# Attention products in plain float32 on halves and strips of the array, two heads at once

## The chip, the cores and the metric

The kernel runs on one core of one Trainium2 chip. The metric is the device time of one execution in microseconds (us). TensorE (PE in the profile) multiplies matrices, VectorE (DVE), ScalarE (ACT) and GpSimd (POOL) work on elements, SyncE (SP) issues the transfers between device memory and the on-chip buffers. PSUM is the on-chip memory that TensorE's products land in; it has eight banks of 512 float32 values on each of 128 partitions.

## The reference

The first stage is a linear attention with a feature map, for 8 batches of 8 heads with 576 tokens, a head width of 64 and 128 features. Its result is reshaped to 4608 tokens of 512 values, and a gated layer with 1536 inner columns follows.

```python
def phi(x):
    proj = np.einsum('bhsd,df->bhsf', x, w_phi)
    proj = proj - np.max(np.abs(proj), axis=-1, keepdims=True)
    return np.concatenate([np.exp(proj), np.exp(-proj)], axis=-1)
q_p, k_p = phi(q), phi(k)
kv = np.einsum('bhsf,bhsd->bhfd', k_p, v)
z = np.sum(k_p, axis=2)
num = np.einsum('bhsf,bhfd->bhsd', q_p, kv)
den = np.einsum('bhsf,bhf->bhs', q_p, z)[..., None] + 1e-06
x = (num / den).transpose(0, 2, 1, 3).reshape(B * S, H * D)
a = x @ w_a
b = x @ w_b
out = a * b @ w_out
```

## The kernel before, in words

The work has two phases. In the first, the attention of 32 pairs of heads (8 batches, 4 pairs each) is interleaved with the first pass of the gated layer, which takes 6 of its 12 slices of inner columns over 12 blocks of 384 tokens (`moe_block`, products at L609 and L632). The second pass (`second_pass`, L722 and L833) takes the other 6 slices in blocks of 768 tokens with a scheme that trades products for sums; it begins when the first pass is done, and the change doesn't touch it. A block of the first pass needs the normalised attention of the tokens in it, from all heads of a batch.

A product can be made in two ways. In plain float32 each product appears in the trace as two records of TensorE, each with a weight load of its own. In the split way an operand is cut into a rounded part and the rest (`split`, `stack`, type float32r), the product is the sum of three products of such parts (`products`), and each has one record. The gated layer is split everywhere. The attention is plain for the first pairs (`PLAIN_K, PLAIN_Q, PLAIN_KV, PLAIN_NUM = 9, 6, 11, 9` at L45: keys up to pair 9, queries up to 6, and so on) and split for the rest. ScalarE and VectorE make the parts (L153, L160, L165).

For a pair of heads the steps are these. `features` projects the keys: 4 chunks of 128 tokens, and a fifth of 64 tokens that two pairs share (`rest_chunk`). In the plain way one product per chunk makes both heads, with a weight matrix that holds w_phi twice and zeros elsewhere, 256 columns (L234); in the split way there are two products per chunk, where the low part lies in the other half of the rows (L243). VectorE takes the largest absolute value and subtracts it (L248, L249), ScalarE makes two exponentials (L257, L258). `kv_add` (L300) multiplies the values by these features and adds over the chunks in one PSUM bank; a column of ones beside the 64 value columns makes z in the same product, so that the stationary operand is 65 columns wide, and 64 in the product of the values' low part. `k_finish` copies the sums out and transposes them by four products (L322). `q_side` does the queries head by head: two products of 288 tokens each (L358), the largest absolute value over the partitions on POOL (L362), exponentials (L366, L367), and products with the transposed sums, numerator and denominator in one, again 65 columns wide (L382). Numerators go to device memory (`xun`), denominators too (`den`). `reciprocals` loads the denominators, inverts them, stores them, loads them again spread over the partitions (`rb`), loads the numerators (`x32` from `xun`), multiplies (L410), and stores `xnorm`, from which the blocks load.

The order of the source is set by turns. `attention_steps` gives each step of a pair a turn (5 turns from pair to pair for the first 7 pairs, 4 after that), sorts the steps by turn, and between turns `run` issues steps of the gated layer and of the weight decoding at 0.65 or 0.75 steps per turn. The instructions of each engine are then put in order by a scheduler with a model of times (`schedule_with_timeline_sim=True`), so TensorE's order isn't that of the source. The four attention buffers in PSUM (tag `att`) are one bank each, three banks belong to the gated layer (tag `moe`), and one to the sums.

## Time and profile before

| what | value |
|---|---|
| median of 3 runs | 1219.85 us |
| lowest and highest run | 1218.25 and 1220.84 us |
| span of the profiled execution | 1218.5 us |
| PE busy | 1182.0 us, 97% |
| DVE busy | 972.3 us, 80% |
| ACT busy | 779.0 us, 64% |
| DMA busy share, from 100 to 694 us | 0.50 |

The span runs from the first instruction to the last of one execution; what the profiled execution took as a whole isn't listed beside it, and the median of the runs is 1.35 us above the span. Attention products run from 4 us to 694 us, products of the first pass from 65 us to 803 us, those of the second pass from 806 us on. TensorE's records are pipelined: the next one starts before the one before it ends, so what a product costs in a row of products is the distance between starts, not the duration of a record.

### The profile page before, as it was taken

Reading aid. Unit: us, or ns where it says so; the run is one execution under the profiler, and the core shown is the slowest. Engines: PE = TensorE matmul, PEld = TensorE weight load, DVE = VectorE, ACT = ScalarE, POOL = GpSimd, SP = SyncE. Lnnn points to the kernel's source line nnn. Section 1 sums busy time; section 2 is a strip of 40 time slices with the busy share of each in tenths; the row PEclk is TensorE's granted clock in tenths of the full one; section 3 lists DMA queues with packets and bytes.
Section 4 is the critical chain, followed back from the end, with each engine's and each line's share of the span. In section 5 each row is a group of like instructions: output and inputs, shape, how many; then the busy total and the mean of one; then the engine's idle time right before and its main releaser. Section 6 shows DMA issues by size and latency. Waiting matters only on the chain.

```text
span 1218.5 us, 20169 instructions
## 1 busy us (share of the span) xinstructions
PE 1182.0 (97%) x7086; PEld 1125.7 (92%) x7086; DVE 972.3 (80%) x1716; ACT 779.0 (64%) x1656; POOL 152.5 (13%) x69
## 2 busy tenths in 40 slices
PE   8889999999999999999999999999999999999998
PEld 5557888999999999999999999999999999998997
DVE  7966988898898889898888479978768595867665
ACT  6767778888888888888788445644345353535332
POOL 2222222121221221131122000000000000000000
PEclk9999999999999999999999999999999999999999
DMA  8665664454455454545341578759586767768572
GB/s 254 206 208 179 181 189 130 133 167 119 140 154 159 116 166 114 161 131 170 108 132 55 168 251 298 236 169 309 174 271 204 232 240 219 257 205 285 169 247 87
DMA packets 120949, 225.21 MB, mean 185 GB/s; under 512 B 21456, under 2 KB 58064, under 8 KB 120848
## 3 DMA queue, kind: packets, MB, share of 16 engines
q1 hardware_dynamic: 120400, 223.66, 59.2%
q8 instruction: 56, 0.92, 0.3%
q14 instruction: 45, 0.37, 0.1%
q10 hardware_dynamic: 448, 0.26, 0.1%
HBM read 174.81 MB, written 49.05 MB: 184 GB/s over the span
## 4 chain that ended last, share of the span: by engine, by line
PE 70%; DMA 13%; DVE 9%; ACT 5%; issue 2%; SPq 0%; DVEq 0%; ACTq 0%
PE po L833 9%; PE pa L722 9%; PE pa L609 9%; PE pb L722 9%; PE pb L609 8%; PE po L632 8%; PE kvps L300 7%; PE pn L382 6%; DMA x<-xnorm 3%; PE pq L358 2%; DMA back_w<-kept_w 2%; DMA xnorm<-x 1%; PE pk L243 1%; DMA rb<-rec 1%; DMA rec<-r 1%
## 5 line engine op out<-in xcount | busy, mean ns | idle before, releaser
L362 POOL PARTITION_ALL_REDUCE mb<-p x64 | 152.2, 2378 | 524.8 <-ACT p L359 412.0
L609 PE MATMUL pa<-xh,w_a 128*128 128x384 f32 x576 | 165.7, 341 | 5.7 <-ACT xh L153 4.1
L609 PE MATMUL pb<-xh,w_b 128*128 128x384 f32 x576 | 161.6, 338 | 0.0
L632 PE MATMUL po<-hh,w_o 128*128 128x384 f32 x576 | 153.1, 337 | 2.0 <-ACT o L644 2.0
L609 PEld LDWEIGHTS pa<-xh,w_a 128*128 128x128 f32 x576 | 105.6, 189 | 8.1 <-ACT xh L153 5.0
L632 PEld LDWEIGHTS po<-hh,w_o 128*128 128x128 f32 x576 | 104.1, 188 | 2.9 <-ACT o L644 2.6
L609 PEld LDWEIGHTS pb<-xh,w_b 128*128 128x128 f32 x576 | 105.0, 188 | 0.3
L609 PE MATMUL pa<-xl,w_a 128*128 128x384 f32 x288 | 98.1, 341 | 0.0
L609 PE MATMUL pb<-xl,w_b 128*128 128x384 f32 x288 | 97.1, 337 | 0.0
L632 PE MATMUL po<-hl,w_o 128*128 128x384 f32 x288 | 96.8, 338 | 0.3 <-DVE hl L160 0.3
L160 DVE TENSOR_TENSOR qel<-qe,qeh 128x1152 fp32r<-128x1152 f32 x46 | 62.9, 1366 | 28.1 <-ACT qeh L153 25.8
L833 PE MATMUL po<-hh_s,own_o 128*128 128x384 f32 x288 | 80.2, 335 | 0.6 <-DVE o L815 0.3
L165 DVE TENSOR_TENSOR qs<-q,qs 64x576 fp32r<-64x576 f32 x52 | 63.1, 1214 | 16.4 <-ACT qs L153 15.2
L383 ACT COPY xn<-pn 65x288 f32<-65x288 f32 x128 | 48.9, 395 | 23.1 <-PE pn L382 17.2
L833 PE MATMUL po<-hh_w,own_o 128*128 128x384 f32 x216 | 59.1, 334 | 0.0
L632 PEld LDWEIGHTS po<-hl,w_o 128*128 128x128 f32 x288 | 54.1, 188 | 0.8 <-DVE hl L160 0.7
L366 ACT ACTIVATE qe<-p 128x576 f32<-128x576 f32 x64 | 44.6, 696 | 15.9 <-DVE qel L160 12.2
L609 PEld LDWEIGHTS pa<-xl,w_a 128*128 128x128 f32 x288 | 54.2, 188 | 0.3
L609 PEld LDWEIGHTS pb<-xl,w_b 128*128 128x128 f32 x288 | 54.2, 188 | 0.3
L153 ACT CAST qeh<-qe 128x1152 fp32r<-128x1152 f32 x46 | 53.5, 1162 | 1.4 <-PE pn L382 1.3
L833 PEld LDWEIGHTS po<-hh_s,own_o 128*128 128x128 f32 x288 | 52.6, 188 | 1.5 <-DVE o L815 0.6
L257 ACT ACTIVATE ke<-kd 128x512 f32<-128x512 f32 x64 | 40.9, 640 | 20.1 <-DVE kd L249 19.4
(299 smaller groups left out, 3422.1 us busy)
## 6 DMA issues: line engine op xcount, KB each, us to landing
back_s<-kept_s SPq DMA_DIRECT2D x71, 512.0 KB
back_w<-kept_w SPq DMA_DIRECT2D x52, 512.0 KB
q<-in_qD SPq DMA_DIRECT2D x52, 288.0 KB
k<-in_km SPq DMA_DIRECT2D x55, 256.0 KB
xun<-xn SPq DMA_DIRECT2D x64, 144.0 KB
x<-xun SPq DMA_DIRECT2D x32, 288.0 KB
rb<-rec SPq DMA_DIRECT2D x32, 288.0 KB
xnorm<-x SPq DMA_DIRECT2D x32, 288.0 KB
```

What stands on the lines that cost most here:

```text
L153: eng.copy(dst, src)
L160: eng_lo.tensor_tensor(lo, src, hi, op=ALU.subtract)
L165: eng_lo.tensor_tensor(hi_lo[D:], src[D:], hi_lo[D:], op=ALU.subtract)
L300: nc.tensor.matmul(st["kv_ps", b, pr][:width, j], v_[:, j, :width], e_[:, j], start=(left == NFULL and j == 0 and n_ == 0), stop=(left == ...
L362: nc.gpsimd.partition_all_reduce(mb, p32, P, bass_isa.ReduceOp.absmax)
L366: nc.scalar.activation(e[:, 0], p32, AF.Exp)
L382: nc.tensor.matmul(pn[: D + 1, :HALF], kv_[:, 2 * j + s, :], e_[:, s, tok], **at)
L383: nc.scalar.copy(xn[: D + 1, tok], pn[: D + 1, :HALF])
L609: nc.tensor.matmul(acc, w[:, cc * P : (cc + 1) * P], x, start=(k == 0), stop=(k == 3 * NCC - 1))
L632: nc.tensor.matmul(accs[cc], w[:, cc * P : (cc + 1) * P], h, **at)
L722: in_turn(lambda: nc.tensor.matmul(acc[to][i], w_, x_, skip_group_check=True, **at), u.startswith("1_0"))
L833: in_turn(lambda: nc.tensor.matmul(acc[m, to], w_, h_, skip_group_check=True, **f), False)
```

## The change

All attention products become plain float32, for all pairs. They are laid on parts of the array. The projections of queries and keys have 64 contracted rows per head, so the two heads of a pair stand on the two halves of the rows (`heads[j]`) and write two PSUM banks. The sums over keys and values and the numerators have 64 output columns per head, so the two heads stand on the two halves of the columns. The column of ones goes: z is made by products with a stationary operand of 32 columns of ones, on four strips of 32 columns for two heads and two signs of the exponent (`strips`), from the features of all chunks for the first 8 pairs, and from their sum, which VectorE makes first (`summed`), for the other 24. Denominators are products of their own, on four strips for two heads and two halves of the tokens (`den_products`). The transposes become three of 128 x 128.

Each step is one function, issued in one turn: `load` at turn -5, `project` at 0, `summed` at 2, `kv_products` and `z_products` at 4, `turn` at 5, `num_products` and `den_products` at 8, with 4 turns between pairs. Steps of the same turn are sorted by kind, so in one turn come `project` of a pair, `kv_products` of the pair before, `num_products` of the one before that, then `z_products` and `den_products`. All products of attention and of the first pass go through `pe`, which ties each to the one before it, so that TensorE runs them in the order of the source. PSUM has two attention buffers of two banks instead of four of one; the sums and their transposes share one bank, and the three banks of the gated layer stay. The numerators of a pair are copied to `x32` on chip and stay there until they are multiplied; `xun` goes. The splits of keys, queries, values and features go, and so do the loads of the doubled queries (`qD`) and of the values with a column of ones. The rows of x come in the order of the heads, and the host lays the weights out to fit.

The core of the diff:

```diff
-TURNS0, TURNS, PAIRS0 = 5, 4, 7
...
+TURNS = 4
+LOAD_TURN, QK_TURN, SUM_TURN, KV_TURN, TURN_TURN, NUM_TURN = -5, 0, 2, 4, 5, 8
+SUM_FROM = 8
...
-PACE0, PACE, PACE0_UNTIL = 0.65, 0.75, 30
+PACE0, PACE, PACE0_UNTIL = 0.65, 0.75, 24
...
-PLAIN_K, PLAIN_Q, PLAIN_KV, PLAIN_NUM = 9, 6, 11, 9
...
-        ps = c.enter_context(tc.tile_pool(name="ps_att", bufs=4, space=PSUM))
+        ps = c.enter_context(tc.tile_pool(name="ps_att", bufs=2, space=PSUM))
...
+    ordered = [None]
+    def pe(issue):
+        ins = issue()
+        if ordered[0] is not None:
+            tc.add_manual_dep(
+                ins.ins,
+                ordered[0].ins.name,
+                mybir.DependencyInfo(mybir.DependencyClass.NoSync, mybir.DependencyReason.DATA),
+                reason="order of products",
+            )
+        ordered[0] = ins
+        return ins
+    def mm(out, w, x, start=True, stop=True):
+        return pe(lambda: nc.tensor.matmul(out, w, x, start=start, stop=stop, skip_group_check=True))
...
+        ones = a1.tile([P, 3, D // 2], F32, name="ones")
+        nc.vector.memset(ones, 1.0)
+        nc.vector.memset(ones[D:, 1], 0.0)
+        nc.vector.memset(ones[:D, 2], 0.0)
...
+    heads = [slice(j * D, (j + 1) * D) for j in range(2)]
+    strips = [slice(i * P // 4, (i + 1) * P // 4) for i in range(4)]
+    times = [slice(t * HALF, (t + 1) * HALF) for t in range(2)]
+    def load(b, pr, a1, a2, ps, consts, st):
         u = f"{b}_{pr}"
+        k32 = a2.tile([P, NFULL * P], F32, tag="k32", name=f"k32_{u}")
+        loads.append(nc.sync.dma_start(k32, km[b, pr]))
+        q32 = a2.tile([P, S], F32, tag="q32", name=f"q32_{u}")
+        loads.append(nc.sync.dma_start(q32, qP[b, pr]))
+        if pr % 2 == 0:
+            g = pr // 2
+            rk = a2.tile([P, P], F32, tag="rk", name=f"rk_{u}")
+            loads.append(nc.sync.dma_start(rk, kr[b, g]))
+            rv = a2.tile([P, 2, 2, D], F32, tag="rv", name=f"rv_{u}")
+            loads.append(nc.sync.dma_start(rv, vr[b, g]))
+            st["rk", b, g], st["rv", b, g] = rk, rv
+        v32 = a2.tile([P, NFULL, 2, D], F32, tag="v32", name=f"v32_{u}")
+        loads.append(nc.sync.dma_start(v32, vm[b, pr]))
+        st["k", b, pr], st["q", b, pr], st["v", b, pr] = k32, q32, v32
+    def features(u, y, n, a1, a2):
+        p = y if n == NFULL else y[:, :, :F]
+        p = p.rearrange("p j (c f) -> p j c f", f=F)
+        tag, bufs = ("d", 2) if n == NFULL else ("dr", 1)
+        d = a1.tile([P, 2, n, F], F32, tag=tag, bufs=bufs, name=f"d_{u}")
+        m = a2.tile([P, 2, n], F32, tag=f"m{n}", name=f"m_{u}")
+        nc.vector.tensor_reduce(out=m, in_=p, op=ALU.max, axis=AX.X, apply_absolute_value=True)
+        nc.vector.tensor_tensor(d, p, m.unsqueeze(3).broadcast_to([P, 2, n, F]), op=ALU.subtract)
+        e = a1.tile([P, 2, n, 2, F], F32, tag=f"e{n}", bufs=1 if n == NFULL else 2, name=f"e_{u}")
+        nc.scalar.activation(e[:, :, :, 0], d, AF.Exp)
+        nc.scalar.activation(e[:, :, :, 1], d, AF.Exp, scale=-1.0)
+        return e
+    def project(b, pr, a1, a2, ps, consts, st):
+        w2 = consts[0]
+        u = f"{b}_{pr}"
+        k32, q32 = st["k", b, pr], st["q", b, pr]
+        p32 = a2.tile([P, 2, S], F32, tag="p32", name=f"p32_{u}")
+        def q_half(t):
+            x = ps.tile([P, 2, 512], F32, tag="att", name=f"pq_{u}_{t}")
+            for j in range(2):
+                mm(x[:, j, :HALF], w2[heads[j]], q32[heads[j], times[t]])
+            return x
+        x = q_half(0)
+        nc.scalar.copy(p32[:, :, times[0]], x[:, :, :HALF])
+        y = ps.tile([P, 2, 512], F32, tag="att", name=f"pk_{u}")
+        for c in range(NFULL):
+            for j in range(2):
+                mm(y[:, j, c * P : (c + 1) * P], k32[heads[j], c * P : (c + 1) * P], w2[heads[j]])
+        x = q_half(1)
+        if pr % 2 == 0:
+            for j in range(2):
+                mm(x[:, j, HALF : HALF + F], st["rk", b, pr // 2][heads[j]], w2[heads[j]])
+        nc.scalar.copy(p32[:, :, times[1]], x[:, :, :HALF])
+        st["e", b, pr] = features(u, y, NFULL, a1, a2)
+        if pr % 2 == 0:
+            st["er", b, pr // 2] = features(f"r_{u}", x[:, :, HALF:], 1, a1, a2)
+        eq = a1.tile([P, 2, 2, S], F32, tag="eq", bufs=2, name=f"eq_{u}")
+        for j in range(2):
+            mb = a2.tile([P, S], F32, tag="mb", name=f"mb_{u}_{j}")
+            nc.gpsimd.partition_all_reduce(mb, p32[:, j], P, bass_isa.ReduceOp.absmax)
+            marks.append(nc.vector.tensor_tensor(p32[:, j], p32[:, j], mb, op=ALU.subtract))
+        nc.scalar.activation(eq[:, :, 0], p32, AF.Exp)
+        nc.scalar.activation(eq[:, :, 1], p32, AF.Exp, scale=-1.0)
+        st["eq", b, pr] = eq
+    def summed(b, pr, a1, a2, ps, consts, st):
+        if b * NPAIR + pr < SUM_FROM:
+            return
+        u = f"{b}_{pr}"
+        e, er = st["e", b, pr], st["er", b, pr // 2]
+        two = a1.tile([P, 2, 2, 2 * F], F32, tag="raw", bufs=2, name=f"two_{u}")
+        ev = e.rearrange("p j c s f -> p j c (s f)")
+        nc.vector.tensor_tensor(two, ev[:, :, 0:2], ev[:, :, 2:4], op=ALU.add)
+        z = st["z", b, pr] = a2.tile([P, 2, 2 * F], F32, tag="z", name=f"z_{u}")
+        nc.vector.tensor_tensor(z, two[:, :, 0], two[:, :, 1], op=ALU.add)
+        rows = heads[pr % 2]
+        rv = er.rearrange("p j c s f -> p j (c s f)")
+        nc.vector.tensor_tensor(z[rows], z[rows], rv[rows], op=ALU.add)
+    def kv_products(b, pr, a1, a2, ps, consts, st):
+        e, er = st["e", b, pr], st["er", b, pr // 2]
+        v32, rv = st["v", b, pr], st["rv", b, pr // 2]
+        kv = st["kv", b, pr] = ps.tile([P, 3, P], F32, tag="kv", bufs=1, name=f"kv_{b}_{pr}")
+        kvs = kv.rearrange("p s f -> p (s f)")
+        for c in range(NFULL):
+            for j in range(2):
+                mm(kvs[heads[j], : 2 * F], v32[:, c, j], e[:, j, c].rearrange("p s f -> p (s f)"), start=(c == 0), stop=False)
+        for j in range(2):
+            mm(kvs[heads[j], : 2 * F], rv[:, pr % 2, j], er[:, j, 0].rearrange("p s f -> p (s f)"), start=False)
+    def z_products(b, pr, a1, a2, ps, consts, st):
+        ones = consts[2]
+        e, er, kv = st["e", b, pr], st["er", b, pr // 2], st["kv", b, pr]
+        js = [(j, s) for j in range(2) for s in range(2)]
+        if ("z", b, pr) in st:
+            for i, (j, s) in enumerate(js):
+                mm(kv[strips[i], 2], ones[:, 0], st["z", b, pr][:, j, s * F : (s + 1) * F])
+            return
+        for c in range(NFULL):
+            for i, (j, s) in enumerate(js):
+                mm(kv[strips[i], 2], ones[:, 0], e[:, j, c, s], start=(c == 0), stop=False)
+        for i, (j, s) in enumerate(js):
+            mm(kv[strips[i], 2], ones[:, 1 + pr % 2], er[:, j, 0, s], start=False)
+    def turn(b, pr, a1, a2, ps, consts, st):
+        ident = consts[1]
+        u = f"{b}_{pr}"
+        back = a2.tile([P, 3, P], F32, tag="back", bufs=1, name=f"back_{u}")
+        nc.scalar.copy(back, st["kv", b, pr])
+        pt = ps.tile([P, 3, P], F32, tag="kv", bufs=1, name=f"pt_{u}")
+        for g in range(3):
+            pe(lambda: nc.tensor.transpose(pt[:, g], back[:, g], ident))
+        kvh = st["kvh", b, pr] = a2.tile([P, 3, P], F32, tag="kvh", name=f"kvh_{u}")
+        nc.vector.tensor_copy(kvh, pt)
+    def num_products(b, pr, a1, a2, ps, consts, st):
+        u = f"{b}_{pr}"
+        kvh, eq = st["kvh", b, pr], st["eq", b, pr]
+        pn = ps.tile([P, 2, 512], F32, tag="att", name=f"pn_{u}")
+        for t in range(2):
+            for s in range(2):
                 for j in range(2):
+                    mm(pn[heads[j], t, :HALF], kvh[:, s, heads[j]], eq[:, j, s, times[t]], start=(s == 0), stop=(s == 1))
+        x32 = st["x", b, pr] = a2.tile([P, S], F32, tag="x32", name=f"x32_{u}")
+        nc.scalar.copy(x32.rearrange("p (t n) -> p t n", t=2), pn[:, :, :HALF])
+    def den_products(b, pr, a1, a2, ps, consts, st):
         u = f"{b}_{pr}"
+        kvh, eq = st["kvh", b, pr], st["eq", b, pr]
+        pd = ps.tile([P, 2, 512], F32, tag="att", name=f"pd_{u}")
+        for s in range(2):
+            for j in range(2):
+                for t in range(2):
+                    mm(pd[strips[2 * j + t], 0, :HALF], kvh[:, 2, strips[2 * j + s]], eq[:, j, s, times[t]], start=(s == 0), stop=(s == 1))
+        dn = a2.tile([P, HALF], F32, tag="dn", bufs=1, name=f"dn_{u}")
+        nc.scalar.copy(dn, pd[:, 0, :HALF])
+        rows = dn.rearrange("(g r) n -> g r n", r=P // 4)[:, 0]
+        nc.sync.dma_start(den[b][2 * pr : 2 * pr + 2].rearrange("h (t n) -> (h t) n", t=2), rows)
...
-        x32 = a1.tile([P, S], F32, tag="x32", name=f"x32_{b}_{pr}")
-        nc.sync.dma_start(x32, xun[b][rows])
...
+        x32 = st["x", b, pr] = a2.tile([P, S], F32, tag="x32", name=f"x32_{u}")
...
+            t0 = TURNS * i
+            args = (b, pr, *pools, consts, st)
+            units = ((load, LOAD_TURN), (project, QK_TURN), (kv_products, KV_TURN), (num_products, NUM_TURN))
+            units += ((z_products, KV_TURN), (den_products, NUM_TURN), (turn, TURN_TURN), (summed, SUM_TURN))
+            for order, (f, t) in enumerate(units):
+                plan(order, once(f, *args), [t0 + t])
...
+        stages.sort(key=lambda x: x[:3])
...
-                        nc.tensor.matmul(acc, w[:, cc * P : (cc + 1) * P], x, start=(k == 0), stop=(k == 3 * NCC - 1))
+                        mm(acc, w[:, cc * P : (cc + 1) * P], x, start=(k == 0), stop=(k == 3 * NCC - 1))
```

## Rows read from the trace of the kernel before

**Rows 1.** The page: busy us by engine; then granted TensorE clock in 40 slices.
```profile
PE 1182.0 (97%) x7086; PEld 1125.7 (92%) x7086; DVE 972.3 (80%) x1716; ACT 779.0 (64%) x1656; POOL 152.5 (13%) x69
...
PEclk9999999999999999999999999999999999999999
```

**Rows 2.** Windows of two stretches: stretch, its length, busy us (instructions), clock, DMA share.
```profile
0.00:65.00 65.00, 55.43 (x238) 36.10 (x239) 53.45 (x97) 44.46 (x94) 17.14 (x13) 1.00 0.74 230
...
100.00:694.00 594.00, 589.37 (x3841) 568.34 (x3839) 510.39 (x777) 486.79 (x1011) 125.56 (x52) 1.00 0.50 143
```

**Rows 3.** Timeline of PE in 108:122: start us, us from first start to last end, records.
```profile
110.22 0.30 PE L358 MATMUL pq<-qs,wh 128*128 128x288 f32 x1
...
110.75 1.13 PE L382 MATMUL pn<-qe,kvh 128*65 128x288 f32 x4
111.72 1.03 PE L300 MATMUL kvps<-ke_r,rvz 128*65 128x256 f32 x4
112.58 1.89 PE L300 MATMUL kvps<-ke,v 128*65 128x256 f32 x8
```

**Rows 4.** Timeline of PE in 207.5:213, products of split keys and values.
```profile
207.99 0.28 PE L300 MATMUL kvps<-keh,vaug 128*65 128x256 f32 x1
208.10 0.28 PE L300 MATMUL kvps<-kel,vaug 128*65 128x256 f32 x1
208.22 0.28 PE L300 MATMUL kvps<-keh,vl 128*64 128x256 f32 x1
208.34 0.28 PE L300 MATMUL kvps<-keh,vaug 128*65 128x256 f32 x1
...
209.40 0.29 PE L358 MATMUL pq<-qs,wh 128*128 128x288 f32 x1
```

**Rows 5.** Chain that ended last, in order of time: start us, us, what.
```profile
66.61 3.92 DMA den<-xn
...
87.33 0.69 PE pa L609
...
103.56 0.24 PE pt L322 x4
```

**Rows 6.** Groups by line on PE: shape, count, busy us, mean ns, idle before.
```profile
L300 PE MATMUL kvps<-keh,vl 128*64 128x256 f32 x168 | 46.9, 279 | 0.0
L300 PE MATMUL kvps<-keh,vaug 128*65 128x256 f32 x168 | 46.9, 279 | 0.0
...
L300 PE MATMUL kvps<-ke,v 128*65 128x256 f32 x176 | 43.5, 383 | 2.5 <-ACT ke L258 2.5
...
L382 PE MATMUL pn<-qe,kvh 128*65 128x288 f32 x144 | 42.2, 424 | 2.2 <-ACT p L359 1.3 <-DVE kd L249 0.4 <-ACT qe L367 0.2
...
L382 PE MATMUL pn<-qeh,kvh 128*65 128x288 f32 x184 | 38.2, 295 | 1.2 <-ACT kvh L325 1.0 <-DVE kd L246 0.3
...
L243 PE MATMUL pk<-wk,ks 128*128 128x256 f32 x184 | 35.1, 287 | 0.0
...
L358 PE MATMUL pq<-qs,wh 128*128 128x288 f32 x104 | 30.7, 307 | 1.4 <-DVE qs L165 1.1 <-DVE kd L246 0.2
```

**Rows 7.** Groups by line on DVE and ACT: shape, count, busy us, mean ns.
```profile
L160 DVE TENSOR_TENSOR qel<-qe,qeh 128x1152 fp32r<-128x1152 f32 x46 | 62.9, 1366 | 28.1 <-ACT qeh L153 25.8 <-PE pq L358 2.2
...
L160 DVE TENSOR_TENSOR kel<-ke,keh 128x1024 fp32r<-128x1024 f32 x42 | 51.2, 1219 | 2.2 <-ACT keh L153 2.0
...
L359 ACT COPY p<-pq 128x288 f32<-128x288 f32 x128 | 45.9, 404 | 5.2 <-PE pq L358 5.2
...
L249 DVE TENSOR_TENSOR kd<-pk,m 128x512 f32<-128x512 f32 x18 | 12.3, 684 | 0.6 <-ACT ke L258 0.3
L248 DVE TENSOR_REDUCE m<-pk 128x4 f32<-128x512 f32 x18 | 12.2, 679 | 6.7 <-PE pk L234 6.6
```

**Rows 8.** Timeline of weight loads (PEld) in 207.5:213, beside rows 4.
```profile
208.10 0.13 PEld L300 LDWEIGHTS kvps<-keh,vl 128*64 128x64 f32 x1
```

More of the change, by code (lines that the diff above doesn't have):

```diff
@@ L83, in tile_kernel @@
     NFULL = S // P
-    REST = P // 2
     HALF = S // 2
@@ L97, in tile_kernel @@
     ps_moe = pstack.enter_context(tc.tile_pool(name="ps_moe", bufs=3, space=PSUM))
-    xun = [dpool.tile([DM, S], F32, name=f"xun{b}") for b in range(B)]
     den = [dpool.tile([H, S], F32, name=f"den{b}") for b in range(B)]
@@ L151, in copy @@
-    def copy(eng, dst, src):
-        if eng is nc.scalar:
-            eng.copy(dst, src)
-        else:
-            eng.tensor_copy(dst, src)
+        busy = a1.tile([P, 2 * S], F32, tag="eq", bufs=2, name="busy")[:, :WARM]
+        nc.vector.memset(busy, 0.0)
+        warm = ps.tile([P, 2, 512], F32, tag="att", name="warm")
+        for _ in range(WARM_TIMES):
+            mm(warm[:, 0, :WARM], busy[:, :P], busy)
+        ones = a1.tile([P, 3, D // 2], F32, name="ones")
+        nc.vector.memset(ones, 1.0)
@@ L267, in k_chunks @@
-    def k_chunks(b, pr, c0, a1, a2, ps, consts, st):
-        u = f"{b}_{pr}"
-        gen = features(f"{u}_{c0}", b * NPAIR + pr, st["k", b, pr][0], c0, 2, a2, ps, consts)
-        yield next(gen)
-        es = next(gen)
-        yield
-        if c0 == 0:
-            pool, tag, bufs = spare(b, ps)
-            st["kv_ps", b, pr] = pool.tile([P, 2, 2 * F], F32, tag=tag, bufs=bufs, name=f"kvps_{u}")
-            st["kv_left", b, pr] = NFULL + 1
-        for c in range(2):
-            kv_add(b, pr, [v_[:, c0 + c] for v_ in st["v", b, pr]], [e_[:, 2 * c : 2 * c + 2] for e_ in es], st)
-        yield
@@ L282, in rest_chunk @@
-    def rest_chunk(b, g, a1, a2, ps, consts, st):
-        gen = features(f"{b}_{g}_r", b * NPAIR + 2 * g, st["rk", b, g][0], 0, 1, a2, ps, consts)
-        yield next(gen)
-        st["re", b, g] = next(gen)
-        yield
-    def rest_add(b, pr, st):
-        kv_add(b, pr, [v_[:, pr % 2] for v_ in st["rv", b, pr // 2]], st["re", b, pr // 2], st)
-        yield
-    def kv_add(b, pr, vs, es, st):
-        left = st["kv_left", b, pr] = st["kv_left", b, pr] - 1
-        for j in range(2):
-            parts = products(vs, es)
-            for n_, (v_, e_) in enumerate(parts):
-                width = D if n_ == 2 else D + 1
-                nc.tensor.matmul(
-                    st["kv_ps", b, pr][:width, j],
-                    v_[:, j, :width],
-                    e_[:, j],
-                    start=(left == NFULL and j == 0 and n_ == 0),
-                    stop=(left == 0 and n_ == len(parts) - 1),
-                    skip_group_check=True,
-                )
@@ L403, in reciprocals @@
         behind(loads, lambda: nc.sync.dma_start(rec[b][hs].rearrange("h (a n) -> (h a) n", n=n), r))
-        x32 = a1.tile([P, S], F32, tag="x32", name=f"x32_{b}_{pr}")
-        nc.sync.dma_start(x32, xun[b][rows])
         yield
-        rb = a1.tile([P, S], F32, tag="rb", name=f"rb_{b}_{pr}")
-        behind(loads, lambda: nc.sync.dma_start(rb, rec[b][hs].unsqueeze(0).broadcast_to([D, 2, S])))
+        rb = a2.tile([P, S], F32, tag="rb", name=f"rb_{b}_{pr}")
+        for j in range(2):
+            behind(loads, lambda: nc.sync.dma_start(rb[heads[j]], rec[b][2 * pr + j : 2 * pr + j + 1].broadcast_to([D, S])))
         yield
+        x32 = st["x", b, pr]
         behind(marks, lambda: nc.vector.tensor_tensor(x32, x32, rb, op=ALU.mult))
```

291 lines of the change are left out of this document (27 added, 264 removed).

## The prediction

> **What bounds the kernel now.** I read the page first: TensorE is busy 97% of the span, and its granted clock is near full in every slice [rows 1]. Then the windows by stage. From 100 to 694 us, where attention and the first pass of the gated layer run together, PE is busy 589.4 of 594 us, while DVE has 510.4, ACT 486.8, and the transfers half of their engines [rows 2]. So there every microsecond of PE time counts, and nothing that is taken from DVE, ACT or the queues counts by itself. Only in the first 65 us does PE have gaps (55.4 busy), with DVE busy 53.5 [rows 2]. The reader should then see in PE's timeline how far apart the starts of records stand, for that is the price of a product. Plain float32, two records each: four records of 288 columns take 111.72 - 110.75 = 0.97 us, 0.2425 each; four of 256 columns 112.58 - 111.72 = 0.86, 0.215 each [rows 3]. Split, one record each: the four records of 288 columns from 110.22 to 110.75 take 0.1325 each [rows 3], the twelve of 256 columns from 207.99 to 209.40 take 0.1175 each [rows 4]. Four transposes take 0.24 [rows 5]. The second pass is left as it is, and so are the 2592 products of the first.
>
> **What attention costs PE before.** A plain pair: keys 8 records x 0.215 + 2 for half of a shared chunk x 0.215/2 = 1.9; queries 8 x 0.2425 = 1.9; sums 20 x 0.215 = 4.3; numerators 16 x 0.2425 = 3.9; transposes 0.24; in all 12.3 us. A split pair: keys 9 x 0.1175 = 1.1; queries 8 x 0.1325 = 1.1; sums 30 x 0.1175 = 3.5; numerators 24 x 0.1325 = 3.2; transposes 0.24; in all 9.1. The four switches come at pairs 9 (keys), 6 (queries), 11 (sums; 12 for the shared chunk) and 9 (numerators), which gives 32 x 9.1 = 290 and, for the plain ones, 9 x 0.9 + 6 x 0.9 + 11.2 x 0.8 + 9 x 0.7 = 28: 318 us. The counts agree: 168 records for each of the three split sums, 21 pairs of 8, 176 plain ones, 11 pairs of 16, 144 plain numerators, 9 pairs of 16, 184 of each split kind, 23 of 8 [rows 6].
>
> **What it costs after.** A record of 128 columns isn't in the trace in plain float32; I take half of 0.215, 0.108. One after the other, a pair would take: queries 8 x 0.2425 = 1.94; keys 16 x 0.108 = 1.73, and 0.22 for half of the shared chunk; sums 20 x 0.215 = 4.30; z 8 x 0.108 = 0.86, but 40 x 0.108 = 4.32 in the first 8 pairs; numerators 16 x 0.2425 = 3.88; denominators 3.88 too; three transposes, wider than before, 0.3. That is 17.1, and 20.6 early: 24 x 17.1 + 8 x 20.6 = 575 us. So everything hangs on how far products on different parts of the array run at once, which no row shows. The bounds:
> - Not at all: 575, +257.
> - Two at a time. Each product is two records in a row on one part of the array; the second can't start before the first has streamed, and in the trace records start in order. So where products of two parts alternate, the second record of one and the first of the other go together, and two records take one record's time. This halves all but the transposes: 8.7 and 10.4 a pair, 24 x 8.7 + 8 x 10.4 = 292, -26. On four strips it stays at two, since the third product waits for the second's first record.
> - Four at a time on the strips, with starts no closer than the 0.06 of the transposes [rows 5]: denominators 16 x 0.06 = 0.97 instead of 1.94, z no better than at two: 292 - 32 x 0.97 = 261, -57.
>
> I take two at a time, since it only asks that the order of starts which the rows show also holds between parts.
>
> The Trainium skill, "TensorE: Matmul & The Clock Gate", Part 3 (Packing small matmuls — row/col tiling), says that products on different parts of the array run at once, that they start and end in program order, and that four row strips measured 3.07 times. By its concurrency and order the sum is the 292 above, by its 3.07 for four parts it lies nearer to the 261. No row here shows either.
>
> **The switches between shapes of tile.** In a period of four turns TensorE goes from the whole array to halves of the rows, halves of the columns, strips, and back: four switches a pair. The nearest row: the sums of split pairs alternate between 65 columns (the whole array) and 64 (which the built program gives a tile of 128 x 64), with starts at 208.10, 208.22 and 208.34, no more time on either side of the narrow one [rows 4]. So I cost a switch at nothing. If the array had to empty instead, each would add what a record lasts beyond the next start, 0.28 - 0.12 = 0.16 us [rows 4]: 4 x 32 x 0.16 = 20 us. The Trainium skill, "TensorEngine Tiling (Array Packing)", Key Properties, says that changing the mode drains TensorE; by that the sum would be 292 + 20, and these rows disagree with it.
>
> **The order and two PSUM buffers.** TensorE now waits wherever the source puts a product too early. In a burst, `q_half(0)`, the keys, `q_half(1)` and the numerators take the two `att` buffers in turn. The numerators of pair i-2 want the buffer of pair i's keys, which DVE reads twice: 2 x 0.68 for the largest value and 2 x 0.68 for the subtraction [rows 7], 2.7 us. Meanwhile PE has `q_half(1)` 0.5, the shared chunk 0.1, and the sums 2.15, also 2.7. So PE waits for the rest of what DVE was at when the keys were done: nothing if DVE is idle, up to some 1.2 us if it has just begun an operation as long as the feature splits [rows 7], more if two stand in line. `q_half(1)` wants the buffer that ACT copies in about 2 x 0.40 [rows 7] while PE has 0.87 of keys: nothing, or the rest of an ACT operation. Behind a waiting product stands everything on PE, the gated layer too. Bounds 0 and 2 us a pair. The splits of features alone are 51.2 + 62.9 of DVE's time [rows 7]; with them and the other splits gone I estimate DVE at 0.6 busy, so 0.6 x half of 1.2 = 0.4: 32 x 0.4 = +13.
>
> **The front.** Until the first block can start PE has only attention. From a pair's denominators to the first product of the block that needs them the chain took 66.61 to 87.33 us, 21 us of transfers with two DVE steps and a cast [rows 5]; `xun` is not on it. The same transfers stay, and PE fills them with the pairs that follow. In these 85 us PE will do seven bursts of 8 to 10 us, as little more or less than it does now. I take 0, bounds -10 and +10.
>
> **At nothing.** DVE gains the additions that make z, estimated at 1.2, 0.6 and 0.6 us from the 1.22 of 1024 columns [rows 7]; ACT and DVE lose the casts and splits. All of it, like the dropped transfers, lies under PE [rows 2]; without that cover the additions would cost 24 x 2.4 = 58. The loads of a pair all go out five turns ahead, over one period, so SP's queue, with fewer transfers in it, isn't late.
>
> **Sum.** 1218.5 - 26 + 13 = 1205.5 of span, and the 1.35 by which the median lies above the span: 1207 us.
>
> **Rivals.**
> - A, the forecast, two at a time: 1207, own range 1190 to 1229. Chance 0.40.
> - B, strips four at a time: 1207 - 31 = 1176. For it: the 0.06 between transposes shows that records can start so close [rows 5]. Against: the two records of each product in order. 0.27.
> - C, slower by the wait for PSUM: its place is the first numerator product of a burst, its price 1.5 us a pair instead of 0.4, +35, 1242. It decides from 26/32 = 0.8 us a pair on. For it: one waiting product holds all of PE. Against: DVE loses much of its load. 0.12.
> - D, the array empties at each switch: +20, 1227. Against it, rows 4. 0.05.
> - E, the weight load of a record doesn't get ahead of the record before it, so that of two records that go together one starts late by 0.06 us, the distance of two transposes [rows 5]: 11.3 and 14.0 a pair, 383, 1207 + 91 = 1298. For it: with the whole array the load for the record at 208.22 starts only at 208.10, with the record before it [rows 4, 8]. Against: there its place in the array wasn't free earlier. 0.09.
> - F, no products at once: 575, 1207 + 283 = 1490. The change wouldn't do what it says. 0.07.
>
> **Numbers.** A is likeliest, so 1207. The range reaches over A, B, C and D, 1155 to 1245, and leaves out E and F (0.16). Below 0.2%, 2.4 us, a measurement of this kernel can't be told from no change. Faster: 0.32 of A, all of B, 0.01 of C: 0.60. Same: 0.04 of A, 0.02 of D: 0.06. Slower: the rest, 0.34.
>
> **What would show it.** In PE's timeline of a burst, starts of sum records 0.108 apart on average mean two at a time (0.215 is F, 0.14 is E); of denominator records 0.12 is A, 0.06 is B. A gap at the start of each kind of product is D. Idle time before `pn` with DVE's subtraction as the one waited for, over 1 us, is C. Attention should end nearer to 680 us than 694. The prediction fails if products on parts of the array don't overlap, or if the fixed order costs more than the overlap gives.

## The result and the profile after

The changed kernel takes 1232.8 us (median of 4 runs, 1232.6 to 1237.1), the kernel before, run beside it, 1219.1: a ratio of 1.0126, 95% interval 1.0094 to 1.0158. It is slower by 1.3%, where 1207 was forecast. Below, a ratio is always to the kernel before, run on the same chip.

The page of the changed kernel, busy time by engine and the granted clock in 40 slices:

```profile
PE 1152.9 (94%) x7974; PEld 1029.8 (84%) x7974; DVE 767.8 (62%) x1411; ACT 561.1 (46%) x1050; POOL 139.9 (11%) x69
...
PEclk9889989999999999999999899999999999999999
```

Against [rows 1], PE's busy time fell by 29.1 us and its idle time rose from 36.5 to 78.1, by 41.6; together the 12.5 us by which the span grew (1218.5 to 1231.0). DVE lost 204 us of busy time and ACT 218, and the span didn't get shorter by it.

Windows of the changed kernel, the stretches of [rows 2] first, columns as there:

```profile
0.00:65.00 65.00, 43.09 (x415) 29.54 (x415) 49.85 (x79) 38.63 (x58) 21.45 (x15) 0.89 0.61 192
...
100.00:694.00 594.00, 561.87 (x4309) 468.34 (x4297) 350.34 (x604) 295.41 (x508) 109.98 (x52) 0.99 0.41 124
```

In the first 65 us PE is busy 43 us instead of 55, while DVE has 50, hardly less than the 53 of before. From 100 to 694 us PE, which had been idle for 4.6 us, is idle for 32.

The timeline of PE in one burst of the changed kernel, which answers to [rows 3, 4]: start, us from the first start to the last end, records, and idle time ahead with what ended it.

```profile
297.45 1.06 PE L106 MATMUL pk<-w,k 64*128 64x128 f32 x16
298.73 0.76 PE L106 MATMUL pq<-q,w 64*128 64x288 f32 x4 [0.23 <-ACT p L179]
299.42 1.95 PE L106 MATMUL kv<-e,v 128*64 128x256 f32 x16
301.20 0.60 PE L106 MATMUL kv<-e_r,rv 128*64 128x256 f32 x4
301.63 2.11 PE L106 MATMUL pn<-eq,kvh 128*64 128x288 f32 x16
303.67 0.42 PE L106 MATMUL kv<-z,ones 128*32 128x128 f32 x8
303.91 1.15 PE L106 MATMUL pd<-eq,kvh 128*32 128x288 f32 x16
304.99 0.45 PE L106 MATMUL pa<-xh,w_a 128*128 128x384 f32 x1
```

The 20 records of the sums take 301.63 - 299.42 = 2.21 us, 0.11 each: on halves two go at a time. The 16 of the denominators take 304.99 - 303.91 = 1.08, 0.067 each, with the change to the whole array in it: on strips four at a time.

What PE waited for in the changed kernel (us in all, times, longest):

```profile
PE pt L248 <- ACT back L245: 18.8, 11, 4.1
PE pn L106 <- DVE d L159: 13.4, 5, 4.7
PE pq L106 <- ACT p L179: 12.1, 19, 2.5
PE po L106 <- ACT hh L127: 4.9, 4, 2.6
PE po L106 <- DVE hl L128: 3.5, 4, 2.2
```

up to 115 us alone:

```profile
PE pt L248 <- ACT back L245: 12.9, 7, 4.1
PE pq L106 <- ACT p L179: 7.8, 5, 2.5
PE pn L106 <- DVE d L159: 4.5, 2, 3.4
```

and the groups of PE, as in [rows 6], for the products inside a burst that waited:

```profile
L106 PE MATMUL pn<-eq,kvh 128*64 128x288 f32 x512 | 74.1, 435 | 17.0 <-DVE d L159 13.4 <-DVE d_r L159 2.4 <-ACT p L188 1.0
...
L106 PE MATMUL pq<-q,w 64*128 64x288 f32 x256 | 50.2, 469 | 13.9 <-ACT p L179 12.1 <-DVE d L159 1.8
...
L106 PE MATMUL pk<-w,k 64*128 64x128 f32 x512 | 36.0, 282 | 3.5 <-DVE d L159 3.5
```

**A budget.** I count from the starts of all PE records what each product takes at the full clock when nothing is in its way (records that go together once: 0.216 us for 256 columns, 0.2425 for 288, 0.109 for 128, 0.173 for the layer's, 0.108 for a transpose; for the kernel before the spacings of the prediction), and what lies beyond it (below: beyond the undisturbed spacing). Attention's share, the warm-up with it, is 320 us before and 251 after, -69.6; the layer's is 448 in both. Time beyond it grows by 84 us up to the second pass, from 37 to 121: +20 in 0 to 65 us (15 to 35), +10 to 115, +15 to 200, +28 from 200 to 600 (6 to 34), and +10 after. (The expectation of experiment 1 has about 42 and 110 for these two totals.) Part of that are changes of tile shape: before the first record of a new shape and its second, the starts stand 0.12 us (halves of the columns to strips), 0.22 (strips to the whole array), 0.20 (to halves of the rows) and 0.15 (from these to halves of the columns) further apart than within one shape: 0.69 a burst, 32 x 0.69 = 22 us. The other 62 are waits and a lower clock.

The granted clock has two levels in these traces, 1.0 and 0.5 (2.4 and 1.2 GHz). A stretch at the lower one:

```profile
81.20:84.40 3.20, 3.20 (x18) 1.86 (x16) 3.20 (x5) 0.95 (x2) 2.16 (x1) 0.50 0.92 305
```

In it two pairs of records of `e_r` take 0.85 us, from 82.85 to the start of `pn` at 83.70; at the full clock they take 301.63 - 301.20 = 0.43. In the first pass of the changed kernel 41 us are at the lower level, and records worth 16.8 us at the full clock start in them; before, it was 7 us with 2.5. So I estimate that the lower clock takes 14 of the 62 us, 7 of them up to 115 us. The second pass starts 84 - 69.6 = some 14 us later (14.2 in the trace, 805.8 to 820.0); it is itself 2 us shorter. That leaves three causes to test: the front, the changes of shape, and the fixed order with its waits.

### The profile page after: what moved, and what is told of

It is laid out like the page before. It is cut to its first block, busy times and chain, and to the rows that moved or that the text cites. A ratio compares the mean times of both kernels' runs of the same rounds, so it can differ in the third digit from the quotient of the medians.

```text
span 1231.0 us, 20665 instructions
## 1 busy us (share of the span) xinstructions
PE 1152.9 (94%) x7974; PEld 1029.8 (84%) x7974; DVE 767.8 (62%) x1411; ACT 561.1 (46%) x1050; POOL 139.9 (11%) x69
## 4 chain that ended last, share of the span: by engine, by line
PE 68%; DMA 13%; DVE 12%; ACT 4%; issue 2%; SPq 1%; POOL 0%; ACTq 0%; DVEq 0%
PE po L106 9%; PE pa L106 9%; PE po L715 9%; PE pa L604 9%; PE pb L106 9%; PE pb L604 9%; PE kv L106 5%; PE pn L106 4%; DMA x<-xnorm 2%; PE pq L106 2%; PE pd L106 2%; DMA xnorm<-x 2%; DMA den<-dn 2%; DMA r<-den 2%; DVE h L496 1%
## 5 line engine op out<-in xcount | busy, mean ns | idle before, releaser
L195 POOL PARTITION_ALL_REDUCE mb<-p x64 | 139.7, 2229 | 435.0 <-ACT p L188 370.0
L106 PE MATMUL pn<-eq,kvh 128*64 128x288 f32 x512 | 74.1, 435 | 17.0 <-DVE d L159 13.4
L127 ACT CAST hh<-h 128x384 fp32r<-128x384 f32 x72 | 36.9, 512 | 100.7 <-DVE h L496 100.0
L496 DVE TENSOR_TENSOR h<-pb,h 128x384 f32<-128x384 f32 x72 | 39.9, 554 | 63.6 <-PE pb L106 63.6
L106 PEld LDWEIGHTS pn<-eq,kvh 128*64 128x64 f32 x512 | 39.6, 146 | 44.7 <-issue 22.9
L106 PE MATMUL kv<-e,v 128*64 128x256 f32 x512 | 64.2, 394 | 0.0
L106 PE MATMUL pq<-q,w 64*128 64x288 f32 x256 | 50.2, 469 | 13.9 <-ACT p L179 12.1
L158 DVE TENSOR_REDUCE m<-pk 128x8 f32<-128x1024 f32 x32 | 39.0, 1217 | 34.8 <-PE pk L106 34.8
L209 DVE TENSOR_TENSOR two<-e 128x1024 f32<-128x1024 f32 x24 | 30.3, 1261 | 48.2 <-ACT e L162 48.2
L298 DVE TENSOR_TENSOR x<-x,rb 128x576 f32<-128x576 f32 x32 | 24.2, 756 | 51.4 <-DMA rb<-rec 48.8
```

What stands on the lines that cost most here:

```text
L106: return pe(lambda: nc.tensor.matmul(out, w, x, start=start, stop=stop, skip_group_check=True))
L127: (eng_hi.copy if eng_hi is nc.scalar else eng_hi.tensor_copy)(hi, src)
L158: nc.vector.tensor_reduce(out=m, in_=p, op=ALU.max, axis=AX.X, apply_absolute_value=True)
L195: nc.gpsimd.partition_all_reduce(mb, p32[:, j], P, bass_isa.ReduceOp.absmax)
L209: nc.vector.tensor_tensor(two, ev[:, :, 0:2], ev[:, :, 2:4], op=ALU.add)
L298: behind(marks, lambda: nc.vector.tensor_tensor(x32, x32, rb, op=ALU.mult))
```

## Experiments

**1. No fixed order.** In `pe`:

```
-        if ordered[0] is not None:
+        if False:
```

> The tie between products is left out, so the scheduler places them; all else as in the changed kernel. In the changed kernel PE's distances between starts beyond those of a full row of products add up to about 110 us until the second pass starts (about 42 in the kernel before). Theory W (waits): most of that is PE standing at a product that the source put too early, with the gated layer's products queued behind it; without the tie the scheduler fills those places, some 30 to 40 us go, near 1195 to 1205. Theory S (switches): the loss is the change of tile shape, 0.1 to 0.2 us each; without the tie gated products fall between attention products, there are more switches and pairs are torn apart, 1240 or more.

Measured: 1218.6 us, 1.000 (0.998 to 1.002). Some 14 us come back, and the kernel is as fast as the one before, not faster: neither theory's time. From 200 to 600 us PE is then full, but the changes of shape there rise from 83 to 195, and the time beyond the undisturbed spacing from 34 to 42 us; the gain lies before 200 us and after 600.

**2. Only the layer's products free.** In `moe_block`, twice, attention stays tied:

```
-                        mm(acc, w[:, cc * P : (cc + 1) * P], x, start=(k == 0), stop=(k == 3 * NCC - 1))
+                        nc.tensor.matmul(acc, w[:, cc * P : (cc + 1) * P], x, start=(k == 0), stop=(k == 3 * NCC - 1))
```

> Only attention products are tied to each other; those of the gated layer are free to go between them. Theory W: the waits before the numerators (18 us in all), before the second query half (16) and of the layer's own products on their casts (20) are filled, 25 to 40 us go, 1193 to 1208, with little more switching. Theory S: the same or slower, 1230 to 1245, since every place that the layer's products enter costs two switches more.

Measured: 1213.8 us, 0.997 (0.995 to 0.999), 19 us less than the changed kernel. The window from 200 to 600 us, of the changed kernel and of this one:

```profile
200.00:600.00 400.00, 388.57 (x3053) 318.02 (x3052) 213.57 (x333) 193.95 (x314) 85.23 (x40) 1.00 0.33 96
```

```profile
200.00:600.00 400.00, 399.84 (x3050) 314.29 (x3047) 214.43 (x338) 196.41 (x315) 85.40 (x40) 1.00 0.32 96
```

PE is full, and yet it has done no more: 3050 records instead of 3053. The layer's products slip into the gaps between attention's, and each time the shape changes twice more: 172 changes in these 400 us instead of 83, and 34 us lie beyond the undisturbed spacing, as many as in the changed kernel. What the free order gains it gains at the edges, from 115 to 200 us (17 to 8 us beyond the spacing) and from 600 us to the end of the pass (14 to 7). The time lies between the two theories: the waits are filled, and part of the gain goes to changes of shape.

**3. The keys last.** The same products with the turn's order reversed:

```
-            units = ((load, LOAD_TURN), (project, QK_TURN), (kv_products, KV_TURN), (num_products, NUM_TURN))
-            units += ((z_products, KV_TURN), (den_products, NUM_TURN), (turn, TURN_TURN), (summed, SUM_TURN))
+            units = ((load, LOAD_TURN), (num_products, NUM_TURN), (kv_products, KV_TURN), (den_products, NUM_TURN))
+            units += ((z_products, KV_TURN), (project, QK_TURN), (turn, TURN_TURN), (summed, SUM_TURN))
```

> Same ties, but within a turn the order is numerators, sums, denominators, z, and the projection of the next pair last, so that the PSUM buffer that VectorE reads twice is next wanted a turn later. The number of switches stays at four a pair. Theory W: the 18 us of waits before the numerators go, and no other wait comes in their place beyond a few us: 1212 to 1222. Theory S: no change, 1230 to 1235. If the front sets the end, no change either.

Measured: 1300.9 us, 1.068 (1.063 to 1.073). PE's waits in this kernel:

```profile
PE pk L106 <- ACT x L261: 45.8, 24, 2.5
PE pq L106 <- ACT dn L272: 15.1, 24, 4.1
PE pn L106 <- DVE kvh L250: 14.9, 6, 4.1
```

The wait for DVE's subtraction is gone, but the keys now want the buffer that ACT copies the numerators from, 1.9 us in 24 bursts. As a remedy it fell, and neither theory's time came out, since another wait took the place of the first; it shows what an order costs that meets one late buffer in every burst while the layer's products are tied behind it.

**4. The heads one after the other.** `j` is made the outermost loop in `kv_products` (the sums without the shared chunk) and `num_products`:

```
-        for c in range(NFULL):
-            for j in range(2):
+        for j in range(2):
+            for c in range(NFULL):
```

> In the sums and the numerators the head is the outermost loop, so that products in a row are on the same half of the array. If two halves really run at once in the changed kernel, this takes it away: a pair's sums cost 20 records of 0.215 instead of 10, its numerators 16 of 0.2425 instead of 8, together 4.1 us more, 32 x 4.1 = 131, near 1360. If the overlap in the trace were only how records are drawn, no change, 1233.

Measured: 1257.6 us, 1.033 (1.028 to 1.038). The timeline of PE in it:

```profile
307.36 2.21 PE L106 MATMUL kv<-e,v 128*64 128x256 f32 x13
309.20 0.43 PE L106 MATMUL kv<-e_r,rv 128*64 128x256 f32 x1
309.41 0.38 PE L106 MATMUL kv<-e,v 128*64 128x256 f32 x1
309.46 0.38 PE L106 MATMUL kv<-e_r,rv 128*64 128x256 f32 x1
309.62 0.38 PE L106 MATMUL kv<-e,v 128*64 128x256 f32 x1
309.68 0.41 PE L106 MATMUL pn<-eq,kvh 128*64 128x288 f32 x1
309.84 0.38 PE L106 MATMUL kv<-e,v 128*64 128x256 f32 x1
```

Without the alternation of the heads the time grows by 25 us only, 0.8 us a pair of the 4.1 that the expectation puts on the loss of all overlap, so that neither of its two times came out; most of the overlap stays. In the source, all sums of the second head stand ahead of the shared chunk (`e_r`), and that ahead of the numerators; here records of `e_r` at 309.20 and of `pn` at 309.68 start before records of the second head's sums at 309.41 and 309.84. Records on different halves don't start in program order.

**5. The keys last, the layer free.** Experiments 2 and 3 together.

> The experiment with the layer's products untied, with the turn's order of the one with the keys last (numerators, sums, denominators, z, projections). Theory M (what the reversed order lost was PE standing still at waits with the layer's products tied behind them): free layer products fill the waits wherever there are any, that is after the front, and some 40 of the 68 us that the reversal cost come back: 1235 to 1255 us, PE busy over 395 of the 400 us from 200 to 600. Theory T (the reversed order makes attention itself late, whatever fills the waits: the projections wait for ACT's copies behind it): attention still ends after 660 us and the time stays over 1280.

Measured: 1209.3 us, 0.992 (0.989 to 0.995), the fastest version of all and faster than both kernels. The same reversal that cost 68 us with the layer's products tied costs none with them free: PE is busy 400.00 of the 400 us from 200 on, against 356.88. Theory M was right, and its size too small.

**6. Six changes of shape.** Experiment 2 with `(z_products, KV_TURN)` ahead of `(num_products, NUM_TURN)`.

> The experiment with the layer's products untied, with z moved between the sums and the numerators, so that a turn passes through six changes of tile shape where it had four; no product is added. Theory S (each change of shape costs TensorE 0.12 to 0.22 us, as the starts in the trace of the changed kernel show): two more changes a pair at 0.12 to 0.15, 32 x 0.27 = +9 us over 1213.8: 1219 to 1225. Rival W (the changes cost nothing, what the trace shows there is waiting for PSUM; z now stands where the numerators waited, 6 us): 1206 to 1213.

Measured: 1211.3 us, 0.993 (0.991 to 0.996), against 0.997 (0.995 to 0.999). The dose was too small: because the layer's products already cut the bursts up, the changes from 200 to 600 us went only from 172 to 181. The time lies where W has it, but with so few changes added it decides nothing about S.

**7. Light decoding.** In `load_weights`, in the changed kernel:

```
-            s, g = yield from decode(load_raw(0, f, nm, stage), u, stage)
+            s, g = yield from light(load_raw(0, f, nm, stage), u, stage)
...
-            nc.vector.tensor_tensor(s, s, hi, op=ALU.subtract)
             yield
-            nc.vector.tensor_tensor(lo, s, g, op=ALU.add)
+            nc.vector.tensor_tensor(lo, s, hi, op=ALU.subtract)
```

where `light` is one activation from the high word into `s`.

> The changed kernel, with the 18 weights of the first pass made by one ACT operation, a copy and one subtraction instead of the decoding (it leaves out the shift, the mask, the scaled product and one of the two additions on DVE; the weights, and so the output, are other numbers). This takes 18 x 2.5 = some 45 us from DVE, 12 of the 18 weights before the first block. Theory V (the front is late because DVE, 75% busy, is at a weight when a pair needs it): the first block's first product comes at 95 to 105 us instead of 115.4, the second pass starts 10 to 15 us earlier, 1217 to 1224 us. Rival L (the front is a chain of latencies through ACT's copies, PSUM and the transfers): first product not before 112, 1229 to 1234.

Measured: 1210.0 us, 0.993 (0.990 to 0.996), 23 us less than the changed kernel; the layer's first product comes at 102.5 us instead of 115.1 (its second record at 102.7 instead of 115.4). Theory V, with a gain larger than it said: the second pass starts 21 us earlier, 12 of them gained up to 115 us, 6 from there to 200 and 3 behind, by the time beyond the undisturbed spacing.

**8. The same in the kernel before.**

> The kernel before, with the light decoding of the weights of the first pass (the same cut as in the changed kernel with light decoding; the weights, and so the output, are other numbers). Theory V2 (only the changed kernel's front is set by DVE; in the kernel before TensorE had 51 of the first 60 us to do, so that DVE's work was mostly under it): 0 to 8 us less than 1219, 1211 to 1219. Rival D2 (the decoding stands on the path of both kernels): 18 to 25 us less, 1194 to 1201.

Measured: 1218.0 us, 1.001 (0.998 to 1.003): nothing. The window to 65 us of the changed kernel with light decoding, and then of the kernel before with it:

```profile
0.00:65.00 65.00, 46.35 (x510) 32.27 (x510) 37.11 (x49) 46.78 (x71) 21.60 (x15) 0.95 0.69 224
```

```profile
0.00:65.00 65.00, 58.34 (x256) 40.48 (x257) 30.25 (x56) 49.13 (x104) 17.62 (x13) 1.00 0.83 268
```

DVE lost 23 of its 53 us in the kernel before and the time stayed; it lost 13 of 50 in the changed one, where more of the pairs' work now fits into this window (510 records of PE instead of 415), and the time fell by 23. The decoding was under TensorE's work before, and stands on the path after. How it does so is seen on DVE in the changed kernel, from 44 us on:

```profile
44.20 0.63 DVE L377 TENSOR_TENSOR w_a<-w_a 128x512 f32<-128x512 f32 x1
44.75 1.21 DVE L158 TENSOR_REDUCE m<-pk 128x8 f32<-128x1024 f32 x1
45.88 0.68 DVE L379 TENSOR_TENSOR w_a<-w_a 128x512 fp32r<-128x512 f32 x1
46.48 0.68 DVE L377 TENSOR_TENSOR w_b<-w_b 128x512 f32<-128x512 f32 x1
47.20 0.69 DVE L379 TENSOR_TENSOR w_b<-w_b 128x512 fp32r<-128x512 f32 x1
47.81 0.42 DVE L355 TENSOR_SCALAR w_a<-w_a 128x512 uint32<-128x512 uint32 x1
48.14 1.22 DVE L159 TENSOR_TENSOR d<-pk,m 128x1024 f32<-128x1024 f32 x1
```

and on ACT and on PE around it:

```profile
52.75 0.67 ACT L354 ACTIVATE w_b<-raw_b 128x512 f32<-128x512 f32 x1 [3.87 <-DVE w_a L379]
...
55.75 0.47 ACT L245 COPY back<-kv 128x384 f32<-128x384 f32 x1
```

```profile
40.85 1.06 PE L106 MATMUL pk<-w,k 64*128 64x128 f32 x16
...
51.06 1.15 PE L106 MATMUL pd<-eq,kvh 128*32 128x288 f32 x16
56.27 0.55 PE L248 MATMUL pt<-ident,back 128*128 128x128 f32 x3 [4.06 <-ACT back L245]
```

The pair's keys came out of PE by 41.9 us. DVE needs 2.43 us for them and is done at 49.4, since operations on the weights stand before and between them. ACT's next activation of a weight waits 3.87 us for DVE, behind it in order stand the exponentials and the copy `back`, and behind that PE, 4.06 us.

**9. No largest value over the keys.** In the changed kernel's `features` the reduction is left out and `m` is a constant tile.

> The changed kernel without the largest value over the keys' projections (a constant is subtracted in its place, so the features are scaled differently); DVE then reads a pair's keys once, for 1.22 us, instead of twice, for 2.44, before their PSUM buffer is free for the numerators. Theory C (the numerators' wait for this buffer, 18.5 us in all between sums and numerators, stops all of PE): the wait falls to under 5 us, and with what it held up in the front the time falls by 14 to 20 us, 1213 to 1219. Rival O (another wait of the same order takes its place, for the copies of ACT above all): the wait falls as much, but the time by under 5 us, 1228 to 1233.

Measured: 1227.6 us, 1.006 (1.004 to 1.008), less than the changed kernel by 5 us between the medians and 8 by the ratios: between the two theories, nearer to rival O. PE's largest waits in it:

```profile
PE pt L250 <- ACT back L247: 24.6, 11, 4.3
...
PE pn L106 <- DVE d L161: 5.5, 2, 3.7
...
PE pq L106 <- ACT p L181: 4.1, 15, 0.7
```

The numerators' wait for the subtraction falls from 13.4 to 5.5 us and that for the queries' copy from 12.1 to 4.1; the wait for `back` grows by 6, and the granted clock of the first 65 us falls from 0.89 to 0.79. So this wait is a cause, worth 5 to 8 us as things stand.

**10 and 11. Some 256 more changes of shape.** Experiment 6 with `SUM_FROM = 32` (run 10), and then with the products of z put between those of the sums (run 11):

```
         for c in range(NFULL):
             for j in range(2):
                 mm(kvs[heads[j], : 2 * F], v32[:, c, j], ...
+            for i, (j, s) in enumerate(js):
+                mm(kv[strips[i], 2], ones[:, 0], e[:, j, c, s], start=(c == 0), stop=False)
```

> The experiment with six changes of shape, with z made straight from the features for all pairs (SUM_FROM 32): DVE's additions for 24 pairs are gone (63 us of its time), TensorE has 32 records more in each of them, four at a time 8 x 0.109 = 0.87 us. It is the base of the run that follows. Where PE bounds: 1211 + 24 x 0.87 = 1232, 1227 to 1235. Were DVE the bound from 200 us on: under 1211.

> The kernel of the run before it, the same products, with those for z put between those for the sums chunk by chunk: five groups on halves and five on strips alternate, so that a pair has 8 more changes between halves of the columns and strips, 256 in all. Theory S (a change costs 0.12 into the strips and 0.17 back, as the starts showed): 8 x 0.145 = 1.16 us a pair; 24 pairs in a stretch in which PE is full give +28 over the run before, with the first 8 up to +37. Rival W (a change costs nothing by itself, or the next product's first record overlaps it): under +6.

Measured: 1235.6 us, 1.014 (1.011 to 1.017), as expected where PE bounds, and 1263.9 us, 1.036 (1.033 to 1.040): 28.4 us more for the same products. (In the order of run 11, two accumulations in one PSUM bank alternate, and the output is other numbers.) The timeline of PE in run 11:

```profile
302.83 0.65 PE L106 MATMUL kv<-e,v 128*64 128x256 f32 x4
303.42 0.43 PE L106 MATMUL kv<-e,ones 128*32 128x128 f32 x8
303.77 0.65 PE L106 MATMUL kv<-e,v 128*64 128x256 f32 x4
304.35 0.43 PE L106 MATMUL kv<-e,ones 128*32 128x128 f32 x8
304.71 0.65 PE L106 MATMUL kv<-e,v 128*64 128x256 f32 x4
```

A chunk takes 303.77 - 302.83 = 0.94 us; undisturbed it is 2 x 0.216 + 2 x 0.109 = 0.65, so that two changes cost 0.29, or 0.12 into the strips and 0.16 back by the starts. 24 pairs x 8 x 0.145 = 28, near the 28.4 measured. From 200 to 600 us alone the trace has 318 changes instead of 183, and 19 us more beyond the undisturbed spacing, 0.14 each; up to 115 us, where PE waits anyway, 57 more changes cost nothing. That two accumulations share a bank isn't what costs: in experiment 6 strips of z are followed by numerators in another bank, and the starts are as far apart, 0.16. Theory S.

**12. A subtraction of each weight on GpSimd.** Experiment 5 with `nc.gpsimd` for the subtraction of `hi`.

> The experiment with the keys last and the layer untied, with one of the five DVE operations of each weight of the first pass (the subtraction of the rounded copy, 0.67 to 0.86 us) moved to GpSimd. 12 of the 18 fall before 115 us: 10 us of DVE's time. Theory V (DVE sets the front): 4 to 9 us less than 1209.3, 1200 to 1205. Rival Q (GpSimd's queue holds up the largest values over the queries, which the numerators wait for): 1209 or more.

Measured: 1250.3 us, 1.026 (1.023 to 1.028), 41 us more than experiment 5. One operation takes 1.3 us there instead of 0.7, and PE's wait for `kvh`, which ends with DVE's copy, grows from 9.9 to 23.8 us; the granted clock of the first 65 us falls from 0.89 to 0.81, that of the next 50 from 0.93 to 0.70. DVE had less to do and the front became longer: it isn't DVE's load alone that sets the front, but the chain through the engines that its operations stand in. Which link of it GpSimd lengthens was not separated.

## Why the prediction was wrong

Its sum was -26 for the overlap, 0 for changes of shape, +13 for stalls, 0 for the front. What the runs showed of each:

- **The overlap, -26 (A).** Halves did go two at a time, but on strips four records start together, so that the reason given for stopping at two fell; and experiment 4 shows starts out of order between halves. Attention's own time, without the warm-up, is 249 us, -69.6; rival B had 261, with z left at two at a time. This term was 44 us too small; with it as measured and the rest as it stands, the forecast would have been 1163. "TensorE: Matmul & The Clock Gate" of the Trainium skill, Part 3, has products on different parts at once, which this trace bears out, and says that they start in program order, which experiment 4 does not bear out.
- **The changes of shape, 0.** This step failed. [rows 4] show 64 columns beside 128 without a gap, and were taken to say that any change is free. The changes of this kernel cost 0.12 to 0.22 us each, 22 us in all. In experiment 2 a step from the whole array to halves of the columns costs 0.15 (25 places), so the alternation in [rows 4] doesn't price it; why it is free there isn't shown. Rival D, with 20, had the size, by the mechanism that an earlier record must end first; that its 1227 came near the measured time is luck, since it had the other terms as the forecast had them. Runs 10 and 11 price the changes on the clock. "TensorEngine Tiling (Array Packing)" of the Trainium skill, Key Properties, says that a change of mode drains TensorE; the 0.12 to 0.22 us agree with that, and only the alternation in [rows 4] does not.
- **The stalls, +13 (C).** The mechanism was there. The waits of `pn`, `pq` and `pk` inside the bursts come to 34 us by the groups of PE (17.0, 13.9 and 3.5), against 7 for their like before. But 21 of the 34 lie up to 115 us, in seven bursts; behind the front it is 13 us, 0.5 a burst, near the 0.4 of the prediction. So the size failed in the front, where DVE was no freer than before. Not in the prediction at all are the waits of `pt` for ACT's copy (19 us, 13 of them in the front), those of the layer's own products for what ACT and DVE make of its results (11 us, most of them from 600 us on), and the lower clock. Of what stands behind a wait the layer was named and not costed; with its products free, 19 us come back (experiment 2). Halving DVE's reads gives 5 to 8 (experiment 9).
- **The front, 0, bounds -10 and +10.** This step failed most, with the budget's +30 up to 115 us (5 of it changes of shape in seven bursts, an estimated 7 the lower clock, the rest waits). The prediction took a saving of PE time as worth its whole size, and put the front at no change because "the same transfers stay". It also read gaps of PE in the first 65 us only, where in the kernel before PE is idle for 10 us of these and for 6 of the next 35. But the eight or so pairs of the front are nearly all plain ones in the kernel before; up to 115 us they had next to no splits to lose. So DVE's load there stayed (53 to 50 us in the first 65) while PE's fell (55 to 43), and the chain over DVE and ACT, which TensorE's work had covered, became the pace. Experiments 7 and 8 show DVE's part in it: the same cut of DVE's work gives 23 us after and nothing before. Of the front's 30 us light decoding takes back 12; what else the front hangs on was not separated.
- **At nothing.** The additions for z and the dropped casts, splits and transfers cost and gave nothing from 200 us on, as said; run 10, with 63 us of DVE's additions gone, follows PE's time alone.

As measured, the terms are -69.6 for the overlap, +30 for the front, 25 x 0.69 = +17 for the changes of the 25 bursts behind it, and 84 - 30 - 17 = +37 for the other waits and the lower clock. So two errors of opposite sign met: the gain was put 44 us too small, the losses 71 us too small. In what they cost the causes overlap: 23 us by light decoding, 19 by the free layer, and either alone removes the loss. What sets the front's pace in detail, DVE's load or the order of ACT's queue, stays open after run 12. One sign that the prediction named tells nothing: attention ended at 606 us and not near 680, but with 249 us of the layer's products ahead of its end where there were 340 before.

## What to carry to other kernels

A saving on the engine that bounds counts only in the stages in which it bounds: split it by stage, and ask of each what else has as much to do there, above all in a front where the cheaper paths are already in use. Products on parts of the array are fast in long rows of one shape; count the changes of shape, 0.12 to 0.22 us each here, before cutting products up or letting others slip in between. Where an order is written out by hand, leave the work that could fill its waits untied: here the same order cost 68 us with the layer tied and nothing with it free.

## What the hardware showed unexpectedly

- Plain float32 products on four strips start within some 20 ns of each other and take the time of one, although each is two records: four records of 288 columns start every 0.2425 us, so that four products take 0.485.
- A half of the array runs ahead of the other by some three or four records, out of the program's order (experiment 4).
- In the front, where PE often stands still, the granted clock is lower: 0.89 on average in the first 65 us against 1.00 before, and 0.79 in experiment 9, which may have lost part of its gain to it. At the lower level, 0.5, two pairs of records take 0.85 us instead of 0.43.
